# Agent attention with a maxout feed-forward layer: other ways to turn the first keys and queries, and another place in PSUM for the first product

## The chip, the cores and the metric

The kernel runs on one core of a Trainium2 chip. The time is the device time of one execution in microseconds (us). Before the change it is 464.83 us, the median of 9 runs that lie between 464.5 and 465.23.

A core has engines that work side by side, each through its own list of instructions in order: TensorE (PE in the profile, with its weight loads as PEld), VectorE (DVE), ScalarE (ACT), GpSimd (POOL) and SyncE (SP), which here only issues DMA transfers. An instruction that needs something from another engine waits for a semaphore, and everything behind it on its engine waits with it.

## The reference

Four batches of 12544 queries, keys and values of width 128 are attended through 49 agent vectors per batch, and a feed-forward layer follows.

```python
def sm(a, b):                       # softmax(scale * a @ b.T)
    ...
a2k = sm(agents, k)                 # 49 x 12544 per batch
agent_v = a2k @ v                   # 49 x 128
q2a = sm(q, agents)                 # 12544 x 49
x = (q2a @ agent_v)                 # 12544 x 128
h = max(x @ w1, x @ w2, x @ w3)     # width 768
out = h @ w_out                     # width 128
```

## The kernel before, in words

**Two streams of work.** Keys and values of a batch must be reduced completely to agent_v before any query of that batch can go on. A *key group* is nine tiles of 128 keys. A *query group*, called s in the code, is eight tiles of 128 queries; there are 49 of them. The keys of batch 0 are read first, alone, in twelve groups (ten of nine tiles and two of four). From then on query group s of one batch is worked on together with a key group of the next batch. The text calls these later key groups by the number s of the query group that hosts them: key group 0 is worked on with query group 0.

**A key group.** `load` issues two DMAs (keys, values; L275). `cast_k` and `cast_v` make bf16 of them (GpSimd, L280 and L287). `turn_k` turns the keys so that the width of 128 lies on the partitions. It does so in one of two ways: nine TensorE transposes into a PSUM tile (L294), which `evacuate` then copies to SBUF with VectorE (L300), or one transposing DMA from SBUF to SBUF issued by SP (L296). Before the change the DMA is used for s = 3 and later. Then follow the scores (L312), their exponentials (ScalarE, L317) and the product with the values (L323). The sums over key groups are kept by VectorE (L335) and, for the later batches, by GpSimd (L342).

**The end of a batch of keys.** `k_tail` divides (`normalise`: for batch 0 a reciprocal and a multiplication on VectorE, L401 and L402, which write avT) and then `product` multiplies agent_v into the weights (L418). For batch 0 that happens in two PSUM tiles. The first holds columns 768 to 1536 and is evacuated by VectorE in two parts, of 256 and 512 columns; the second holds columns 0 to 768 and is evacuated in one piece (all L423). The result is G, the weights that the queries see.

**A query group.** The queries are loaded (L474), cast (L478), turned by eight TensorE transposes (L483) and evacuated (`evacuate`, L489; for query group 0 the first half is done by ScalarE on L491). Scores (L504) and exponentials (L510) follow. For each of six slices f of the hidden width there are first(f), called u, and second(f), called v: two matmuls each on L530. `relu_first` (a, ScalarE, L545, or L542 for f = 3) and `max_second` (x, VectorE, L555, or ScalarE on L553 for f = 3) make r of them. The output is accumulated on L560 and L569, scaled by VectorE (L576) and stored (L583). The names u0, v0, a0, x0 below are these steps for slice 0.

**PSUM.** Two rings of PSUM tiles set much of the order. The ring "uv" has three tiles of two banks: products, turned keys and every u and v take one. The ring "om" has two tiles of one bank: turned queries, scores, the host tile of the key group and the outputs. A new tile waits until the reader of an older one is done.

**The order.** It is written out by hand: every step is given a key by `at`, and `emit` goes through them by key (six units of key for one query group) and puts off what lacks a predecessor or a tile. The tables KEY, LATE, BORDER and BEGIN hold the keys. `last_key` is the key of the last key group of batch 0. The order of SP's DMAs is given by the same keys. A semaphore is used again after eight DMAs, so at most eight are under way.

`keep_busy` (L254) issues matmuls whose result is not used.

Of the kernel before, what the change touches and what calls it, by code (L numbers as in the profile page):

```python
# [16 lines left out]
def kernel(  # L17
# [18 lines left out]
    nc = tc.nc  # L36
# [227 lines left out]
    def k_group(b, t0, n, key, s):  # L264

        d = {}
        early = s is None
        K = None if early else table(s)
        if s == 0:
            key += BEHIND  # L270

        def load():
            for name, src in (("k", k), ("v", v)):
                t = d[name] = load_tile()
                nc.sync.dma_start(t[:, :n, :], src[b, t0 * P:(t0 + n) * P, :].rearrange(  # L275
                    "(p j) c -> p j c", j=n))

        def cast_k():
            d["kb"] = work.tile([P, KT, C], BF16, tag="k_bf", bufs=3, name="k_bf")
            nc.gpsimd.tensor_copy(out=d["kb"][:, :n, :], in_=d["k"][:, :n, :])  # L280

        def cast_v():
            d["vb"] = work.tile([P, KT, C], BF16, tag="v_bf", bufs=4, name="v_bf")
            if early:
                nc.scalar.activation(d["vb"][:, :n, :], d["v"][:, :n, :], AF.Copy)  # L285
            else:
                nc.gpsimd.tensor_copy(out=d["vb"][:, :n, :], in_=d["v"][:, :n, :])  # L287

        def turn_k():
            d["kT"] = work.tile([P, KT, P], BF16, tag="kT", bufs=3, name="kT")  # L290
            if early or s < 3:
                t = d["kT_ps"] = uv_tile(BF16).rearrange("p i c -> p (i c)")
                for j in range(n):
                    nc.tensor.transpose(t[:, j * P:(j + 1) * P], d["kb"][:, j, :], ident)  # L294
            else:
                nc.sync.dma_start_transpose(out=d["kT"][:, :n, :],  # L296
                                            in_=d["kb"][:, :n, :].rearrange("p j c -> p (j c)"))

        def evacuate():
            nc.vector.tensor_copy(out=d["kT"][:, :n, :].rearrange("p j c -> p (j c)"),  # L300
                                  in_=d["kT_ps"][:, :n * P])

        def scores():
            if early:
                d["pair"] = uv_tile()
                d["s"] = d["pair"][:, 0, :]
                last_tile["t"] = d["s"]
            else:
                d["s"] = host[s]
            t = d["s"]  # L310
            for j in range(n):
                nc.tensor.matmul(t[:, j * A:(j + 1) * A], d["kT"][:, j, :], agT[:, b, :A],  # L312
                                 start=(j == 0), stop=True, skip_group_check=True)

        def exps():
            d["e"] = work.tile([P, KT * A], BF16, tag="e_k", bufs=3, name="e_k")
            nc.scalar.activation(d["e"][:, :n * A], d["s"][:, :n * A], AF.Exp, scale=scale)  # L317

        def values():
            t, c = (d["pair"][:, 1, :], 0) if early else (d["s"], CV)  # L320
            for j in range(n):
                e = d["e"][:, j * A:(j + 1) * A]
                nc.tensor.matmul(t[:, c:c + A], d["vb"][:, j, :], e, start=(early and j == 0),  # L323
                                 stop=True, skip_group_check=True)
                if early:
                    nc.tensor.matmul(t[:, A:2 * A], ones_bf, e, start=False, stop=True,
                                     skip_group_check=True)

        def add_values():
            w = 2 * A if early else A  # L330
            src = d["pair"][:, 1, :w] if early else d["s"][:, CV:CV + A]
            if t0 + n == NT and not early:
                nc.vector.tensor_tensor(out=avT[:, b, :A], in0=src, in1=Vacc[b], op=ALU.add)
            elif t0:
                nc.vector.tensor_tensor(out=Vacc[b], in0=src, in1=Vacc[b], op=ALU.add)  # L335
            else:
                Vacc[b] = work.tile([P, w], FP32, tag=f"Vacc{w}", name="Vacc")
                nc.vector.tensor_copy(out=Vacc[b], in_=src)

        def add_exps():  # L340
            if t0:
                nc.gpsimd.tensor_tensor(out=Eacc[b][:, :n * A], in0=Eacc[b][:, :n * A],  # L342
                                        in1=d["e"][:, :n * A], op=ALU.add)
            else:
                Eacc[b] = work.tile([P, KT * A], FP32, tag="Eacc", name="Eacc")
                nc.gpsimd.tensor_copy(out=Eacc[b], in_=d["e"])

        if early:
            g = ("early", t0)
            at(key - 30, load)  # L350
            at(key - 5, cast_k)
            at(key - 4, cast_v)
            at(key, turn_k, ("kt", g), (), "uv", [("kt_out", g)])
            at(key + 0.5, evacuate, ("kt_out", g), [("kt", g)])

            last = [("normalise", 0)] if t0 + n == NT else []
            late = max(0, (key - last_key) / 6 + 2)
            at(min(key + 6.6, last_key + 0.58 + 0.02 * late), scores, ("ks", g), [("kt_out", g)],
               "uv", [("ka", g)] + last)
            at(min(key + 7, last_key + 0.64 + 0.01 * late), exps, ("ke", g), [("ks", g)])  # L360
            done = last_key + (0.6 + 0.1 * late if late >= 1 else 0.55)
            at(min(key + 13.2, done), values, ("kv", g), [("ke", g)])
            at(min(key + 13.6, done + 0.01), add_values, ("ka", g), [("kv", g)])
        else:
            at(6.0 * s - 24.6, load)
            at(max(6.0 * s - 12.6, last_key - 3.4 + 0.2 * s), cast_k, ("k_cast", s))
            at(max(6.0 * s - 10.6, last_key - 3.3 + 0.2 * s), cast_v, ("v_cast", s))
            if s > 2:
                at(max(key - 9.1, last_key - 3.2), turn_k, ("kt_out", s), [("k_cast", s)])
            else:  # L370

                turn = 6.0 * s - 3.3 if s else KEY["v0"] + 0.01
                at(turn, turn_k, ("kt", s), (), "uv", [("kt_out", s)])
                at(turn + 0.05, evacuate, ("kt_out", s), [("kt", s)])
            at(key + K["ks"], scores, ("ks", s), [("kt_out", s), ("ho", s)])
            at(key + K["ke"], exps, ("ke", s), [("ks", s)])
            at(key + K["ke"] + 1.5, add_exps, ("kx", s), [("ke", s)])
            at(key + K["kv"], values, ("kv", s), [("ke", s), ("v_cast", s)])
            at(key + K["ka"], add_values, ("ka", s), [("kv", s)])

    def k_tail(b, sum_key, keys, s):
# [25 lines left out]
        def product(c0, *ends):  # L407

            t = uv_tile().rearrange("p i c -> p (i c)")
            a = c0  # L410
            for z in ends:
                cuts = sorted({a, z} | {c for c in (c0 + 512, C1O) if a < c < z})
                for lo, hi in zip(cuts, cuts[1:]):
                    for h in range(2):


                        c = lo + (C if lo >= C1O and h == 0 else 0)
                        nc.tensor.matmul(t[h * H:(h + 1) * H, lo - c0:hi - c0], avT[:, b, :],  # L418
                                         wall[:, c:c + hi - lo], start=True, stop=True,
                                         skip_group_check=True)  # L420
                src = t[:, a - c0:z - c0]
                if s is None:
                    nc.vector.tensor_copy(out=G[b][:, a:z], in_=src)  # L423
                else:
                    nc.scalar.activation(G[b][:, a:z], src, AF.Copy, scale=r_ag[:, b:b + 1])
                a = z
# [24 lines left out]
    def q_group(s):  # L451
# [33 lines left out]
        def evacuate():  # L485
            d["qT"] = work.tile([P, GT, P], BF16, tag="qT", bufs=3, name="qT")
            qT = d["qT"].rearrange("p j c -> p (j c)")
            half = 0 if s else GT // 2 * P
            nc.vector.tensor_copy(out=qT[:, half:], in_=d["qT_ps"][:, half:])  # L489
            if not s:  # L490
                nc.scalar.activation(qT[:, :half], d["qT_ps"][:, :half], AF.Copy)  # L491

        K = table(s)
        q_dma = s >= SB or s + 1 in tails
# [99 lines left out]
        if s == 0:  # L594
            at(last_key - 29.9, load)
            at(last_key - 3.5, cast)
            at(last_key + 0.76, turn_q, ("qt", 0), (), "om", [("qe", 0)])
            at(last_key + 0.77, evacuate, ("qe", 0), [("qt", 0)])
            at(last_key + 0.94, scores, ("s", 0), [("qe", 0)], "om", [("ex", 0)])
            at(last_key + 0.941, exps, ("ex", 0), [("s", 0)])  # L600
        elif not q_dma:
            at(key - 26, load)
            at(max(key - 12.8, last_key - 3.45 + 0.2 * s), cast, ("q_cast", s))
            put("qt", turn_q, ("q_cast", s), ring="om", frees=[("qe", s)])
            put("qe", evacuate, ("qt", s), *([("s", s - 3)] if s >= 3 else []))
# [114 lines left out]
```

The softmax here doesn't subtract the row's maximum and nothing guards it: scores larger than these inputs give would overflow.

## Time and profile before

The profiled execution took 464.95 us. Its span, from the first to the last instruction, is 463.2 us.

| quantity | value | where it is read |
|---|---|---|
| time, median of 9 runs | 464.83 us | the runs |
| profiled execution, and its span | 464.95 us, 463.2 us | the profile |
| TensorE busy | 437.7 us, 95% of the span | busy time of each engine |
| VectorE, ScalarE, GpSimd busy | 402.9, 396.2, 171.8 us | the same |
| granted TensorE clock, mean | 0.999 | clock of the core |
| keys turned by TensorE, evacuated on L300 | 15 groups, 10.7 us busy | costliest groups |
| keys turned by DMA on L296 | 30 | DMA issues |

A row of the timeline reads: start in us, duration in us, engine, line, operation, output and input tile, shapes, count. In brackets stands the time for which the engine was idle before it, and what ended that. Rows that follow each other on one engine may overlap by some hundredths of a us. A row of several instructions spans all of them. "SPq" is the time that SP spends on issuing a DMA; the time to landing is counted from the issue to the last byte.

### The profile page before, as it was taken

To read this page: it belongs to the slowest core of one execution; us is meant where nothing else is said; L and a number is where in the kernel's file an instruction comes from. 1 tells how busy PE (TensorE), PEld (TensorE's weight loads), DVE (VectorE), ACT (ScalarE), POOL (GpSimd) and SP (SyncE) were. 2 spreads that over 40 slices of the span, in tenths; PEclk is the share of its full clock that TensorE was granted. 3 is DMA by queue.
4 is the path that set the end of the run, shared out by engine and by line. 5 is a ranking of instruction groups with operands and counts; after the bars stand their busy time and mean duration, and the time that the engine had idled before them with its cause. 6 is when DMAs were issued, how large, how long until landed. Compare 5 with 4: busy or idle time off the path is not lost.

```text
span 463.2 us, 13350 instructions
## 1 busy us (share of the span) xinstructions
PE 437.7 (95%) x5473; PEld 274.3 (59%) x5473; DVE 402.9 (87%) x512; ACT 396.2 (86%) x460; POOL 171.8 (37%) x179
## 2 busy tenths in 40 slices
PE   2597899999999999999999999999999999999995
PEld 2465466666665666666656666666656555555554
DVE  3255899999988999999989999999988999999995
ACT  3465889989899899899999998998999999999991
POOL 2244963553452545536272446353240101000000
PEclk9999999999999999999999999999999999999999
DMA  8999999996999999997987999996666486644122
GB/s 311 408 411 391 409 363 323 348 323 135 323 291 304 314 266 333 292 269 226 328 306 254 281 330 295 279 266 189 174 138 187 133 193 151 174 123 124 60 93 92
DMA packets 81449, 118.26 MB, mean 255 GB/s; under 512 B 55207, under 2 KB 56683, under 8 KB 81387
## 3 DMA queue, kind: packets, MB, share of 16 engines
q1 hardware_dynamic: 81184, 117.30, 83.1%
q8 instruction: 43, 0.70, 0.6%
q14 instruction: 19, 0.16, 0.1%
q10 hardware_dynamic: 203, 0.10, 0.1%
HBM read 78.74 MB, written 25.69 MB: 225 GB/s over the span
## 4 chain that ended last, share of the span: by engine, by line
PE 80%; DMA 8%; DVE 4%; ACT 4%; issue 2%; SPq 0%; POOL 0%; DVEq 0%; ACTq 0%
PE uv_ps L530 34%; PE o_ps L569 29%; PE o_ps L560 6%; DMA st<-in_k_dram 5%; PE m_ps L483 4%; PE m_ps L504 3%; DVE r L555 3%; ACT a_sb L545 2%; DMA st<-in_q_dram 2%; DMA st<-in_v_dram 2%; PE m_ps L323 2%; PE m_ps L312 1%; PE m_ps L518 1%; DVE o_sb L576 1%; ACT uv_ps L542 0%
## 5 line engine op out<-in xcount | busy, mean ns | idle before, releaser
L555 DVE TENSOR_TENSOR r<-uv_ps,a_sb 128x1024 bf16<-128x1024 f32 x245 | 297.2, 1220 | 14.7 <-PE uv_ps L530 6.5
L545 ACT ACTIVATE a_sb<-uv_ps 128x1024 bf16<-128x1024 f32 x245 | 240.8, 1026 | 14.9 <-PE uv_ps L530 13.6
L530 PE MATMUL uv_ps<-e_q,G 49*128 49x512 bf16 (+3 forms) x1248 | 187.2, 368 | 2.5 <-ACT uv_ps L542 0.7
L569 PE MATMUL o_ps<-wo_bf,r 128*128 128x128 bf16 x2352 | 175.3, 220 | 0.2 <-DVE r L555 0.2
L569 PEld LDWEIGHTS <-r 128*128 128x128 bf16 x2352 | 137.8, 98 | 40.1 <-issue 38.2
L530 PEld LDWEIGHTS <-G 49*128 49x128 bf16 x1248 | 57.8, 93 | 65.3 <-issue 33.1
L342 POOL TENSOR_TENSOR Eacc<-Eacc,e_k 128x441 f32<-128x441 f32 (+1 forms) x30 | 30.5, 1016 | 129.4 <-ACT e_k L317 129.4
L576 DVE TENSOR_TENSOR o_sb<-o_ps,recips 128x512 f32<-128x512 f32 x98 | 67.5, 689 | 9.2 <-PE o_ps L569 6.4
L478 POOL CAST q_bf<-st 128x1024 bf16<-128x1024 f32 x49 | 51.0, 1042 | 60.8 <-DMA qT<-q_bf 59.4
L553 ACT ACTIVATE r<-uv_ps 128x1024 bf16<-128x1024 f32 x49 | 50.2, 1024 | 18.0 <-PE uv_ps L530 17.7
L280 POOL CAST k_bf<-st 128x1152 bf16<-128x1152 f32 (+2 forms) x45 | 50.7, 1127 | 27.4 <-DMA st<-in_k_dram 25.2
L542 ACT ACTIVATE uv_ps<-uv_ps 128x1024 f32<-128x1024 f32 x49 | 49.6, 1012 | 1.7 <-issue 1.3
L560 PE MATMUL o_ps<-G,e_q 128*128 128x256 bf16 x196 | 38.1, 276 | 0.3 <-DVE o_sb L576 0.3
L287 POOL CAST v_bf<-st 128x1152 bf16<-128x1152 f32 (+1 forms) x33 | 37.5, 1136 | 0.6 <-DMA st<-in_v_dram 0.6
L510 ACT ACTIVATE e_q<-m_ps 128x512 bf16<-128x512 f32 x49 | 29.8, 608 | 0.5 <-PE m_ps L504 0.5
L300 DVE COPY kT<-uv_ps 128x1152 bf16<-128x1152 bf16 (+1 forms) x15 | 10.7, 712 | 16.6 <-PE uv_ps L294 16.6
L285 ACT ACTIVATE v_bf<-st 128x1152 bf16<-128x1152 f32 (+1 forms) x12 | 12.9, 1073 | 13.4 <-DMA st<-in_v_dram 13.2
L560 PEld LDWEIGHTS <-e_q 128*128 128x128 bf16 x196 | 12.5, 97 | 19.0 <-issue 17.8
L489 DVE COPY qT<-m_ps 128x1024 bf16<-128x1024 bf16 (+1 forms) x33 | 22.2, 673 | 0.9 <-PE m_ps L483 0.9
L483 PEld LDWEIGHTS <-q_bf 128*128 128x128 bf16 x264 | 14.9, 98 | 13.3 <-issue 10.6
L483 PE MATMUL m_ps<-ident,q_bf 128*128 128x128 bf16 x264 | 20.4, 220 | 0.6 <-POOL q_bf L478 0.6
L504 PE MATMUL m_ps<-qT,agT 128*64 128x512 bf16 (+3 forms) x104 | 19.9, 388 | 0.5 <-ACT qT L491 0.5
(71 smaller groups left out, 226.9 us busy)
## 6 DMA issues: line engine op xcount, KB each, us to landing
st<-in_q_dram SPq DMA_DIRECT2D x46, 512.0 KB, 5.0
out_dram<-o_sb SPq DMA_DIRECT2D x46, 512.0 KB, 3.4
st<-in_k_dram SPq DMA_DIRECT2D x40, 576.0 KB, 6.6
st<-in_v_dram SPq DMA_DIRECT2D x40, 576.0 KB, 7.9
st<-in_k_dram SPq DMA_DIRECT2D x3, 512.0 KB, 5.6
st<-in_v_dram SPq DMA_DIRECT2D x3, 512.0 KB, 7.2
wst<-in_moe_w_dram SPq DMA_DIRECT2D x3, 384.0 KB, 10.5
st<-in_q_dram SPq DMA_DIRECT2D x2, 384.0 KB, 4.8
```

Source lines behind the costliest of these rows:

```text
L280: nc.gpsimd.tensor_copy(out=d["kb"][:, :n, :], in_=d["k"][:, :n, :])
L287: nc.gpsimd.tensor_copy(out=d["vb"][:, :n, :], in_=d["v"][:, :n, :])
L478: nc.gpsimd.tensor_copy(out=d["qb"], in_=d["q"])
L483: nc.tensor.transpose(t[:, j * P:(j + 1) * P], d["qb"][:, j, :], ident)
L530: nc.tensor.matmul(t[:, h, j0 * P:j1 * P], G[b][h * H:h * H + A, col + f * P:col + (f + 1) * P], d["e"][h * H:h * H + A, j0 * P:j1 * P], s ...
L542: nc.scalar.activation(u, u, AF.Relu)
L545: nc.scalar.activation(a_sb[f], u, AF.Relu)
L553: nc.scalar.activation(r, v_ps[f], AF.Relu)
L555: nc.vector.tensor_tensor(out=r, in0=v_ps[f], in1=a_sb[f], op=ALU.max)
L560: nc.tensor.matmul(t[:, i * 2 * C:(i + 1) * 2 * C], d["e"][:, jj * P:(jj + 1) * P], G[batch[jj]][:, C1O:C1O + 2 * C], start=(i == 0), stop ...
L569: nc.tensor.matmul(t[:, c:c + C], r_sb[f][:, h, jj * P:(jj + 1) * P], wo_bf[:, f, :], start=False, stop=True, skip_group_check=True)
L576: nc.vector.tensor_tensor(out=d["out"][:, j:j + m, :], in0=d["o", o].rearrange("p (j c) -> p j c", c=C), in1=d["r"][:, j:j + m].unsqueeze( ...
```

## The change

Five places are edited.

1. Key group 2 is turned by DMA and no longer by TensorE and VectorE. The order number of its DMA is 2.9, which puts it on SP's list behind the value load of key group 3.
2. Key group 0 is still turned by TensorE, but at `last_key + 1.05`. This is behind the two products and ahead of u0 of query group 0; before, it stood behind v0.
3. The loads of query, key and value groups 4 and 5 get later order numbers. On SP the list after the value load of key group 3 was: query 4, keys 4, values 4, query 5, keys 5, values 5, transpose 3. It becomes: transpose 2, query 4, keys 4, values 4, transpose 3, query 5, keys 5, values 5. From query 6 on the list is as it was.
4. The TensorE transposes of query group 0 stand behind the value matmuls of the last key group of batch 0 and no longer ahead of them. The evacuation of all 1024 columns is one ScalarE instruction; before, it was 512 columns on VectorE and 512 on ScalarE.
5. The first product of batch 0 is put into its PSUM tile 256 columns further on. The first part (256 columns) ends the first bank, and the second part (512 columns) fills the second bank; it is one pair of matmuls of 512 columns, where two pairs of 256 were.

```diff
 def turn_k():
-            if early or s < 3:
+            if early or s < 2:
     ...
 else:
-            at(6.0 * s - 24.6, load)
+            at(max(6.0 * s - 24.6, 6.0 * s - 21.05 if s in (4, 5) else -99), load)
     ...
-            if s > 2:
+            if s > 1:
                 at(max(key - 9.1, last_key - 3.2), turn_k, ("kt_out", s), [("k_cast", s)])
             else:
-                turn = 6.0 * s - 3.3 if s else KEY["v0"] + 0.01
+                turn = 2.7 if s else last_key + 1.05
                 at(turn, turn_k, ("kt", s), (), "uv", [("kt_out", s)])
                 at(turn + 0.05, evacuate, ("kt_out", s), [("kt", s)])
     ...
 def product(c0, *ends):
             t = uv_tile().rearrange("p i c -> p (i c)")
+            at0 = c0 if len(ends) == 1 else ends[0] - 512
             a = c0
             for z in ends:
-                cuts = sorted({a, z} | {c for c in (c0 + 512, C1O) if a < c < z})
+                cuts = sorted({a, z} | {c for c in (at0 + 512, C1O) if a < c < z})
     ...
-                        nc.tensor.matmul(t[h * H:(h + 1) * H, lo - c0:hi - c0], avT[:, b, :],
+                        nc.tensor.matmul(t[h * H:(h + 1) * H, lo - at0:hi - at0], avT[:, b, :],
     ...
-                src = t[:, a - c0:z - c0]
+                src = t[:, a - at0:z - at0]
     ...
 def evacuate():                          # of a query group
-            half = 0 if s else GT // 2 * P
-            nc.vector.tensor_copy(out=qT[:, half:], in_=d["qT_ps"][:, half:])
-            if not s:
-                nc.scalar.activation(qT[:, :half], d["qT_ps"][:, :half], AF.Copy)
+            if s:
+                nc.vector.tensor_copy(out=qT, in_=d["qT_ps"])
+            else:
+                nc.scalar.activation(qT, d["qT_ps"], AF.Copy)
     ...
 if s == 0:
-            at(last_key + 0.76, turn_q, ("qt", 0), (), "om", [("qe", 0)])
-            at(last_key + 0.77, evacuate, ("qe", 0), [("qt", 0)])
+            at(last_key + 0.802, turn_q, ("qt", 0), (), "om", [("qe", 0)])
+            at(last_key + 0.803, evacuate, ("qe", 0), [("qt", 0)])
 elif not q_dma:
-            at(key - 26, load)
+            at(key - (21.08 if s in (4, 5) else 26), load)
```

## The prediction

> **What bounds the kernel now.** First the page's head, then the busy time by stage: the hand-over from the keys of batch 0 to the first queries (41.3 to 51.0), the first query groups (51.0 to 62.6), and later groups.
>
> ```profile
> span 463.2 us, 13350 instructions
> PE 437.7 (95%) x5473; PEld 274.3 (59%) x5473; DVE 402.9 (87%) x512; ACT 396.2 (86%) x460; POOL 171.8 (37%) x179
> ...
> core 0: us, PE busy (x) PEld busy (x) DVE busy (x) ACT busy (x) POOL busy (x), PEclk, DMA share, GB/s
> 41.30:51.00 9.70, 7.43 (x85) 3.80 (x81) 6.52 (x12) 4.80 (x7) 7.62 (x8) 1.00 1.02 408
> 51.00:60.00 9.00, 8.13 (x101) 4.49 (x99) 7.80 (x12) 8.11 (x12) 8.17 (x9) 1.00 1.02 409
> 71.00:79.35 8.35, 8.35 (x109) 5.33 (x110) 8.01 (x11) 7.63 (x10) 4.19 (x4) 1.00 1.13 304
> ```
>
> From about 63 us a query group takes 8.35 us and TensorE is busy for all of it. No edit touches a group after s = 3, so nothing is won there: a stretch that TensorE fills is only moved as a whole. The change can win where TensorE stands idle, in the 21 us from 41.3 to 62.7. There the chain of waits and the timeline say what ends each wait:
>
> ```profile
> 42.68 0.44 DVE qT L489
> ...
> 43.14 0.61 ACT qT L491
> ...
> 44.42 0.43 DVE G L423
> ...
> 47.99 0.76 DVE L300 COPY kT<-uv_ps 128x1152 bf16<-128x1152 bf16 x1 [1.09 <-PE uv_ps L294]
> 48.66 1.21 DVE L555 TENSOR_TENSOR r<-uv_ps,a_sb 128x1024 bf16<-128x1024 f32 x1
> 49.24 1.01 ACT L542 ACTIVATE uv_ps<-uv_ps 128x1024 f32<-128x1024 f32 x1 [1.31 <-issue]
> 51.66 0.66 PE L294 MATMUL uv_ps<-ident,k_bf 128*128 128x128 bf16 x9 [0.34 <-DVE r L555]
> ...
> 61.32 0.76 DVE L300 COPY kT<-uv_ps 128x1152 bf16<-128x1152 bf16 x1 [0.79 <-PE uv_ps L294]
> 61.99 0.68 DVE L576 TENSOR_TENSOR o_sb<-o_ps,recips 128x512 f32<-128x512 f32 x1
> 62.73 0.39 PE L560 MATMUL o_ps<-G,e_q 128*128 128x256 bf16 x2 [0.27 <-DVE o_sb L576]
> 63.83 0.39 PE L312 MATMUL m_ps<-agT,kT 128*128 128x49 bf16 x9
> ```
>
> Two spots are seen. At 47.99 VectorE gets to the keys of group 0 only after 1.09 idle, x0 stands behind them (48.66), and ScalarE waits 1.31 for u3. At 61.32 VectorE waits 0.79 for the keys of group 2, evacuates them, and only then scales the output (61.99) for which TensorE waits at 62.73.
>
> **The change part by part.** Times are places in the trace of before.
>
> *First queries.* They arrive as before: the cast ends at 41.96, the eight transposes at 42.64. The two halves of the evacuation run one after the other (0.42 and 0.60), to 43.74. One ScalarE instruction of 128x1024 takes 1.02 by the row of L553: 42.68 to 43.70. The scores start at 43.76 and not 43.79. The values of the last key group move from 42.48 to about 41.3, so VectorE has avT long before it is needed; before, it came at 44.02, just ahead of the product at 44.08. The product follows the scores by 0.22 (512 columns): 43.98, so 0.09 is won.
>
> *First product.* Its first part is evacuated from 44.33 to 44.75. The second part waited 0.5 for that evacuation before (44.42 plus 0.43, then TensorE at 44.90). Here the Trainium skill speaks: PSUM — Partial Sum Buffer, section "PSUM bank collisions raise a hardware error", has PSUM guarded by bank and quadrant. In another bank the second part then needs no wait. But in the program as built it still carries one: for VectorE's instruction behind the one that writes avT, which is this evacuation. I go by the program: TensorE at 44.81 (44.75 plus the 0.05 of a semaphore), end 45.22, evacuations of 512 and 768 columns from 45.24 and 45.85 (0.69 and 0.95 by their rows), end 46.79. Without the wait these would start about 0.5 earlier.
>
> *Keys of group 0.* The nine transposes stand behind the second product, which ends issuing at 45.35; the cast of these keys ends at 44.81 (43.66 plus 1.15), so they need not wait. On PSUM's ring u0 and u1 now take the tiles of the products, so u0 waits for the evacuation that ends at 45.93, and a0 starts at 46.40 where it was 45.99. This loss of 0.41 lies in ScalarE's idle 1.31: a1 ends at 48.34 instead of 47.93, and u3, no longer behind two fillers and eight transposes, is there at 48.15. So a3 starts at 48.36 (was 49.24). VectorE copies the keys at 46.73 without a wait, v0 takes their tile at 47.54, and x0 starts at 47.95 (was 48.66). x0 decides: behind it stand the evacuation of query group 1, x1, and the keys of group 1 at 51.66, which wait for x1. All move by 0.71. ScalarE gains 0.88 at a3 and is held to the same by these keys, whose tile u5 takes. **First sum: 0.7.** It is 0.3 if some wait in this chain has been missed by me (the 0.41 of a0 not hidden), 1.2 if the second part doesn't wait.
>
> *Keys of group 2.* Nine matmuls (nine weight loads from 60.56, so 0.48 of TensorE's issue) and one VectorE copy of 0.76 go. VectorE is free at 60.53 and TensorE's part for L576 ends at 60.78, so the scaling runs 60.8 to 61.5 and L560 can go at 61.5 (was 62.73). u4 and v2 of query group 1 follow at once. But v4 needs the tile of a4, and ScalarE is full from 59.74: x3, a2, a4 (1.02, then 2.01 for two) end at 62.65. So v4 goes at 62.67 where it was 63.27 (the second pair of 63.06). From there TensorE is without a gap, with u0 of the next group held by a5 at 64.17 (due at 64.2). **Second sum: 0.6.** Its ends: 0.3 (ScalarE's wait of 0.33 at a5 is all that is won) and 0.75 (x4 and x5 gain more).
>
> *The DMAs.* These rows are issues of SP, with the time to landing of the two transposes:
>
> ```profile
> 54.55 0.33 SPq L275 DMA_DIRECT2D st<-in_v_dram  x1
> 57.22 5.24 SPq L296 DMA_TRANSPOSE kT<-k_bf  x1
> 67.43 2.10 SPq L296 DMA_TRANSPOSE kT<-k_bf  x1
> ...
> DMA to landing us min/median/max: 9.6/9.6/9.6
> ...
> DMA to landing us min/median/max: 7.7/7.7/7.7
> ```
>
> Transpose 2 waits for its cast (51.90 plus 1.15) and so goes at 53.1; SP, behind the value load of 46.28, holds back query 4 (47.71 before) until then. By that time the eight loads under way still have to 57.3 to go (loads of this stretch land after about 11 us), so the DMA engines don't run dry. What a transpose adds to them: the first landed at 66.8, 1.15 after the load ahead of it (54.55 plus 11.1); the second at 75.1, 2.46 after the store ahead (66.97 plus 5.7). The skill's Advanced Engine Details and Errata, section "X-Bar Transpose (TRN2)", calls transposes as fast as plain DMAs: 295 KB at 410 GB/s would be 0.72, an estimate. The rows count, 1.15 to 2.46. So transpose 2 lands at 58.5 to 59.8, and its scores, at 63.83 before, are due at 62.5. It pushes all behind it by 1.15 to 2.46: query 4 lands near 60.0 (cast at 59.21 before, used 15 us later), keys 4 near 61.4 (cast by 62.6; GpSimd's list keeps its order, and behind that cast stands L342, due at 63.8 where it was 65.09), transpose 3 at 64 to 66 (due 70.9), transpose 4 at 76.3 to 77.6 instead of 75.1 (its scores, 80.53 before, are due at 79.2). By the page's figure it would be 75.9. Price nothing; least cover 1.6.
>
> *Sum.* 0.7 + 0.6 = 1.3 off the span of 463.2: 461.9. The profiled execution lies 1.75 above its span, and 0.12 above the median: 463.65 and **463.5 us** for the median, 0.28% below 464.83. Within 0.2% (0.93 us) a measurement of this kernel can't be told from no change.
>
> **The rivals.**
>
> *The wait between the product's parts is gone after all.* For it: the second part lies in another bank. Against: the wait in the program. VectorE starts the 512 columns at 44.75 (not 45.24): first sum 1.2, time 463.0.
>
> *Only one spot pays.* ScalarE has 8.11 of 9.00 busy between the spots; if a0's 0.41 or the order of tiles isn't hidden, the first sum is 0 to 0.3 with the second 0.3 to 0.6. Against it: the idle 1.31 on ScalarE behind a1. Time about 464.2, no change by measure.
>
> *Transpose 2 comes too late*, the case on the other side. TensorE holds its whole list at the scores of key group 2, and later groups can't win it back. It costs its landing less 62.5. At 63.83 both gains are gone, which is 10.7 in flight after 53.1; from 64.8 (11.7) on it is slower by more than 0.2%. For it: 9.6 in flight for the transpose of 57.22, behind seven loads, and 11 for loads of this stretch. Against: only three or four loads are ahead of it. At 12.0 in flight, in the middle of this case, it lands at 65.1, costs 2.6 and the time is 466.1. The same loss falls at 80.53 if two transposes take five us more of the DMA engines than seen.
>
> **How the numbers follow.** The sum as worked out 0.50; no wait between the parts 0.12; one spot only 0.22; late transpose 0.16, two thirds of it slower by over 0.2%, else no change. With the edge of the likeliest (0.8 to 1.7, so 463.1 to 464.0) a little of it falls within 0.2% too: faster 0.60, same 0.28, slower 0.12. The range for 8 in 10 goes from 462.8, below the gone wait, to 465.2, into the late transpose.
>
> **What would show it.** Right: x0 (L558 then) near 47.95 and a3 near 48.36, a0 later than before near 46.40, no L294 row behind 52, lin1 of query group 0 (L560, L563 after) near 61.5 less 0.7, so 60.8, the scores of key group 2 without a wait for a DMA, and 8.35 per group behind that. Wrong: TensorE starts the product's second part ahead of 44.8, or waits at L312 on a DMA of kT near 62 or 79, or GpSimd's casts wait for queries 4 or 5 long enough to hold up the sums of L342.

## The result and the profile after

The changed kernel takes 463.34 us (median of 10 runs, 462.89 to 464.45); the kernel before, run beside it, takes 464.92 us (30 runs). The ratio is 0.9966, with a 95% interval of 0.9958 to 0.9974: faster by 0.34%. The forecast was 463.5 us, in a range of 462.8 to 465.2. A second measurement of the changed kernel, told below, gave 463.38 us and 0.9967 (0.9955 to 0.9979).

The profiled execution after took 463.36 us. These are the head of its page and its busy time by engine, and then the busy time in the same three stretches as before (columns as in the prediction):

```profile
span 461.6 us, 13325 instructions
...
PE 437.1 (95%) x5462; PEld 273.8 (59%) x5462; DVE 402.5 (87%) x510; ACT 396.7 (86%) x460; POOL 171.7 (37%) x179
```

```profile
core 0: us, PE busy (x) PEld busy (x) DVE busy (x) ACT busy (x) POOL busy (x), PEclk, DMA share, GB/s
41.30:51.00 9.70, 7.34 (x87) 3.84 (x84) 6.76 (x12) 6.04 (x8) 7.61 (x8) 1.00 1.02 409
51.00:60.00 9.00, 8.34 (x98) 4.77 (x98) 7.67 (x12) 7.93 (x12) 7.72 (x9) 1.00 1.11 341
71.00:79.35 8.35, 8.35 (x112) 5.33 (x110) 8.01 (x11) 7.63 (x10) 4.19 (x4) 1.00 1.11 334
```

The busy time has hardly changed: TensorE has 0.6 us less, VectorE 0.4. The span is 1.6 shorter, so most of what went is idle time of TensorE. The later groups take 8.35 us as before, with TensorE busy for all of it. The timeline after, with the rows that answer to those shown of before:

```profile
46.37 1.94 ACT L548 ACTIVATE a_sb<-uv_ps 128x1024 bf16<-128x1024 f32 x2 [1.70 <-PE uv_ps L533]
46.59 0.75 DVE L300 COPY kT<-uv_ps 128x1152 bf16<-128x1152 bf16 x1
...
48.09 1.23 DVE L558 TENSOR_TENSOR r<-uv_ps,a_sb 128x1024 bf16<-128x1024 f32 x1 [0.75 <-PE uv_ps L533]
...
48.28 1.01 ACT L545 ACTIVATE uv_ps<-uv_ps 128x1024 f32<-128x1024 f32 x1
...
51.11 0.66 PE L294 MATMUL uv_ps<-ident,k_bf 128*128 128x128 bf16 x9 [0.54 <-DVE r L558]
...
60.27 0.69 DVE L579 TENSOR_TENSOR o_sb<-o_ps,recips 128x512 f32<-128x512 f32 x1 [0.29 <-PE o_ps L572]
...
61.04 0.39 PE L563 MATMUL o_ps<-G,e_q 128*128 128x256 bf16 x2
...
62.12 0.39 PE L533 MATMUL uv_ps<-e_q,G 49*128 49x512 bf16 x2 [0.36 <-ACT a_sb L548]
...
62.67 0.39 PE L312 MATMUL m_ps<-agT,kT 128*128 128x49 bf16 x9
```

VectorE's idle 1.09 ahead of the keys of group 0 is gone (46.59 has no bracket), and ScalarE's 1.31 ahead of a3 too (48.28). But x0, which sets what follows, starts at 48.09 and behind a new idle time of 0.75: VectorE now has the keys early and waits for v0. The keys of group 1, which wait for x1, follow at 51.11 (51.66 before). In the second spot the scaling no longer stands behind a key copy, and lin1 starts at 61.04 (62.73 before). The scores of key group 2 (62.67) have no bracket: they wait for no DMA. v4 at 62.12 is held by a4, as the prediction said.

The chain of waits after, in the first spot (start, duration, what):

```profile
44.19 0.44 DVE G L426
...
44.67 0.42 PE uv_ps L421 x2
...
45.11 1.57 DVE G L426 x2
...
46.72 0.39 PE uv_ps L533 x2
47.12 0.54 PE m_ps L254 x2
47.65 0.34 PE uv_ps L533 x2
...
48.09 1.23 DVE r L558
```

The second part of the product (44.67) still waits for the first part's evacuation (44.19 to 44.63). Behind the evacuations the chain does not go through the key copy. It goes through TensorE's list: u1 (46.72), two matmuls of `keep_busy` (47.12), v0 (47.65), x0.

Where the time went, by the starts of the exponentials of query groups (the row of e_q), in two profiled executions of each kernel:

| stretch, us | before | before again | after | after again |
|---|---|---|---|---|
| span start to group 0 | 44.23 | 44.37 | 44.08 | 44.00 |
| group 0 to 1 (first spot) | 9.38 | 9.38 | 8.98 | 8.98 |
| group 1 to 3 (second spot) | 17.84 | 17.85 | 17.23 | 17.21 |
| group 3 to 46 | 355.06 | 355.15 | 354.76 | 354.74 |
| group 46 to 48 | 15.73 | 15.72 | 15.72 | 15.72 |
| group 48 to the end | 20.96 | 20.83 | 20.83 | 20.85 |

The two spots give 0.40 and 0.61 to 0.63. Another 0.3 to 0.4 lies between groups 3 and 46, where no step was edited (0.3 of it in two groups, told at the end of the experiments). The rest lies at the end and in when the first queries arrive, which differs by a tenth or more from one execution to the next (they landed at 40.87 in the profile of before and at 40.76 in that of after).

### The profile page after: what moved, and what is told of

Same layout as the page of the kernel before. It is cut to its first block, busy times and chain, and to the rows that moved or that the text cites. A ratio compares the mean times of both kernels' runs of the same rounds, so it can differ in the third digit from the quotient of the medians.

```text
span 461.6 us, 13325 instructions
## 1 busy us (share of the span) xinstructions
PE 437.1 (95%) x5462; PEld 273.8 (59%) x5462; DVE 402.5 (87%) x510; ACT 396.7 (86%) x460; POOL 171.7 (37%) x179
## 4 chain that ended last, share of the span: by engine, by line
PE 80%; DMA 8%; DVE 5%; ACT 4%; issue 1%; SPq 0%; POOL 0%; DVEq 0%; ACTq 0%
PE uv_ps L533 34%; PE o_ps L572 29%; PE o_ps L563 6%; DMA st<-in_k_dram 5%; PE m_ps L486 4%; DVE r L558 4%; PE m_ps L507 3%; ACT a_sb L548 2%; DMA st<-in_q_dram 2%; DMA st<-in_v_dram 2%; PE m_ps L323 2%; PE m_ps L312 1%; PE m_ps L521 1%; DVE o_sb L579 0%; DVE G L426 0%
## 5 line engine op out<-in xcount | busy, mean ns | idle before, releaser
L533 PE MATMUL uv_ps<-e_q,G 49*128 49x512 bf16 (+3 forms) x1248 | 186.7, 368 | 2.6 <-DVE G L426 0.4
L572 PE MATMUL o_ps<-wo_bf,r 128*128 128x128 bf16 x2352 | 175.3, 220 | 0.2 <-DVE r L558 0.2
L572 PEld LDWEIGHTS <-r 128*128 128x128 bf16 x2352 | 137.8, 98 | 40.0 <-issue 38.1
L533 PEld LDWEIGHTS <-G 49*128 49x128 bf16 x1248 | 57.7, 93 | 64.7 <-issue 32.9
L556 ACT ACTIVATE r<-uv_ps 128x1024 bf16<-128x1024 f32 x49 | 50.2, 1024 | 18.0 <-PE uv_ps L533 17.7
L492 DVE COPY qT<-m_ps 128x1024 bf16<-128x1024 bf16 x32 | 21.8, 681 | 0.0
```

The source lines that it names most:

```text
L533: nc.tensor.matmul(t[:, h, j0 * P:j1 * P], G[b][h * H:h * H + A, col + f * P:col + (f + 1) * P], d["e"][h * H:h * H + A, j0 * P:j1 * P], s ...
L556: nc.scalar.activation(r, v_ps[f], AF.Relu)
L572: nc.tensor.matmul(t[:, c:c + C], r_sb[f][:, h, jj * P:(jj + 1) * P], wo_bf[:, f, :], start=False, stop=True, skip_group_check=True)
```

## The experiments

**One part of the change alone.** Three kernels, each the kernel before with one edit. The first has edits 1 and 3, so the keys of group 2 by DMA and the new order of loads.

```diff
-            if early or s < 3:
+            if early or s < 2:
     ...
-            at(6.0 * s - 24.6, load)
+            at(max(6.0 * s - 24.6, 6.0 * s - 21.05 if s in (4, 5) else -99), load)
     ...
-            if s > 2:
+            if s > 1:
     ...
-            at(key - 26, load)
+            at(key - (21.08 if s in (4, 5) else 26), load)
```

> The kernel before with the keys of group 2 turned by DMA and the loads of groups 4 and 5 behind it, nothing else. The reckoning (two separate gains): 0.6 us faster than before; all starts up to 59 us as before, lin1 of query group 0 (L560) near 61.5 and no longer 62.7, exponentials of query group 3 0.6 us earlier. If the two spots are not separate but one gain seen twice: nothing, or all of the 1.6 us, here. If the DMA order costs something: less than 0.3 us.

Measured: 463.7 us beside 464.78, ratio 0.9977 (0.997 to 0.9984). In the trace the second spot is shorter by 0.63 (17.21), and the first as before (9.38). The time fell by 1.08, where 0.6 was expected: 0.45 more than the stretch explains.

The second has edit 2 for group 0 alone.

```diff
-                turn = 6.0 * s - 3.3 if s else KEY["v0"] + 0.01
+                turn = 6.0 * s - 3.3 if s else last_key + 1.05
```

> The kernel before with the transposes of key group 0 put ahead of u0, nothing else. The reckoning: 0.4 to 0.6 us faster; a0 later by 0.4 (near 46.4), u3's relu (L542) earlier by 0.8, x0 near 48.2 and no longer 48.66. If the later a0 isn't hidden by ScalarE's idle 1.3 us: no change or slower by up to 0.4 us.

Measured: 464.7 us beside 464.78, ratio 1.0001 (0.9993 to 1.0009). The trace has a gain in its place, 9.06 for the first spot (0.32 less, where 0.4 to 0.6 was expected), but the time does not show it. Two groups far behind, 15 and 39, are longer by 0.23 and 0.36 in this trace, and two that are long in the kernel before (0.14 and 0.16) are not: together 0.29 lost, which all but takes up the 0.32. Why is told with the last experiment.

The third has edit 4 alone, the first queries.

```diff
-            half = 0 if s else GT // 2 * P
-            nc.vector.tensor_copy(out=qT[:, half:], in_=d["qT_ps"][:, half:])
-            if not s:
-                nc.scalar.activation(qT[:, :half], d["qT_ps"][:, :half], AF.Copy)
+            if s:
+                nc.vector.tensor_copy(out=qT, in_=d["qT_ps"])
+            else:
+                nc.scalar.activation(qT, d["qT_ps"], AF.Copy)
     ...
-            at(last_key + 0.76, turn_q, ("qt", 0), (), "om", [("qe", 0)])
-            at(last_key + 0.77, evacuate, ("qe", 0), [("qt", 0)])
+            at(last_key + 0.802, turn_q, ("qt", 0), (), "om", [("qe", 0)])
+            at(last_key + 0.803, evacuate, ("qe", 0), [("qt", 0)])
```

> The kernel before with the first queries turned behind the last values and evacuated by one ScalarE instruction, nothing else. The reckoning: 0.1 us or less; VectorE writes avT near 42.7 and no longer 44.0, but the product stays behind the scores on TensorE (near 44.0). If the path runs over VectorE and avT: more than 0.5 us faster.

Measured: 464.66 us beside 464.78, ratio 0.9999 (0.9991 to 1.0008): no change to be measured. In the trace the exponentials of group 0 start 3.32 after the landing of the queries (3.36 before), and the first spot takes 9.30 (9.38): 0.12 together. So at equal arrival the first spot is worth 0.32 + 0.12 = 0.44, and the second 0.61 to 0.63. The changed kernel itself agrees: 3.32 from the landing to the exponentials of group 0, and 8.98 for the first spot, 0.04 and 0.40 less than before.

**The banks.** The changed kernel with the first product back at its old place in PSUM (edit 5 undone).

```diff
-            at0 = c0 if len(ends) == 1 else ends[0] - 512
+            at0 = c0
```

> The changed kernel with the first product at its old place in PSUM (two pairs of 256 columns, the first of them in the bank that VectorE reads). The reckoning: the time of the changed kernel within 0.1 us, because the wait for the first part's evacuation is there in both. If the other bank is what wins: 0.5 us slower than the changed kernel, and TensorE's idle time ahead of the second part shows only here.

Measured: 463.13 us, ratio 0.9968 (0.9956 to 0.998), not to be told from the changed kernel. Its chain of waits:

```profile
44.06 0.43 DVE G L426
...
44.54 0.42 PE uv_ps L421 x4
```

The second part starts 0.48 after the start of the first evacuation, here in the same bank; in the changed kernel, in another bank, it is also 0.48 (44.19, 44.67). Both spots are as long as in the changed kernel (8.98 and 17.21). The place within the tile is worth nothing. The next kernel puts the first part into a PSUM tile of its own, from the other ring.

```diff
+            first = t if len(ends) == 1 else small_tile("m_ps")
     ...
-                        nc.tensor.matmul(t[h * H:(h + 1) * H, lo - at0:hi - at0], avT[:, b, :],
+                        nc.tensor.matmul((first if z == ends[0] else t)[h * H:(h + 1) * H, lo - at0:hi - at0], avT[:, b, :],
     ...
-                src = t[:, a - at0:z - at0]
+                src = (first if z == ends[0] else t)[:, a - at0:z - at0]
```

> The changed kernel with the first part (256 columns) of the first product in a PSUM tile of its own, so that nothing makes the second part wait for its evacuation. The reckoning: TensorE has the second part 0.1 us behind the first and not 0.6; VectorE's copies of 512 and 768 columns, u1, v0, x0 and all behind it move by 0.5 us; 0.5 us faster than the changed kernel. If another chain (ScalarE's from a0, or the keys of group 1) holds x0: less than 0.2 us.

Measured: 462.89 us, ratio 0.9957 (0.9944 to 0.9969). Its chain of waits:

```profile
44.20 1.90 DVE G L426 x3
...
46.14 0.39 PE uv_ps L533 x2
46.53 0.54 PE m_ps L254 x2
47.07 0.34 PE uv_ps L533 x2
...
47.50 1.23 DVE r L558
```

The three evacuations now run as one piece of 1.90, and VectorE waits for TensorE nowhere between them; x0 starts at 47.50, and the first spot takes 8.38: 0.60 less than in the changed kernel. In the changed kernel the second part lies in another bank of the same tile and waits; in another tile it does not. So the wait goes with the tile, not with the bank.

**The fillers.** The changed kernel without the two matmuls of `keep_busy` between u1 and v0.

```diff
-    for key, n in fillers + [(last_key + 0.9, 2), (KEY["u1"] + 0.01, 2),
+    for key, n in fillers + [(last_key + 0.9, 2),
```

> The changed kernel without the two matmuls of no use that stand between u1 and v0 of query group 0. The reckoning: v0 then waits for the copy of the keys of group 0, which ends at 47.34, and starts at 47.4 and not 47.6; 0.2 us faster than the changed kernel. If the two matmuls were needed to hold TensorE's clock: a granted clock under 1.00 behind 46 us and a slower kernel.

Measured: 463.1 us, ratio 0.9966 (0.9953 to 0.9978). Its chain of waits, in an execution in which the first evacuation started 0.22 later than in the changed kernel's (44.41, 44.19):

```profile
45.33 1.55 DVE G L426 x2
46.88 0.68 DVE kT L300
...
47.60 0.41 PE uv_ps L533 x2
...
48.10 1.23 DVE r L558
```

Now the chain goes through the key copy (46.88), and v0 follows its end. x0 starts 3.69 after the first evacuation (3.90 in the changed kernel), and the first spot takes 8.78, 0.20 less. The timed difference (0.24) lies within the intervals; the trace settles it. The granted clock stays at 1.00 from 41 to 60 us, so in this execution the fillers were not needed for it.

**Both together.** The own tile, and no fillers.

> The changed kernel with both: the first part in its own tile, and no matmuls of no use between u1 and v0. The reckoning: the gains add, 0.6 to 0.7 us faster than the changed kernel, 2.0 to 2.3 us faster than before. If one chain holds both: no more than 0.5.

Measured: 462.67 us, ratio 0.9954 (0.9941 to 0.9966): the lowest time of all. The first spot takes 8.20, 0.78 less than in the changed kernel: 0.60 and 0.20 add up.

**The changed kernel again.**

> The changed kernel once more. By the two gains that the traces show (0.44 and 0.63, with the same arrival of the first queries): 1.1 us faster than before. By the first measurement: 1.6 us. What is beyond 1.1 lies outside the edited stretch and should show as differences in single executions, not at one place.

Measured: 463.38 us, ratio 0.9967 (0.9955 to 0.9979), with the same stretches (table above).

**Where transpose 2 stands on SP's list.** The changed kernel with edit 3 undone: the transpose of the keys of group 2 stands behind query 4, keys 4 and values 4.

```diff
-            at(max(6.0 * s - 24.6, 6.0 * s - 21.05 if s in (4, 5) else -99), load)
+            at(6.0 * s - 24.6, load)
     ...
-            at(key - (21.08 if s in (4, 5) else 26), load)
+            at(key - 26, load)
```

> The changed kernel with the loads of key groups 4 and 5 and of the queries 4 back at their earlier places: on SP's list the transpose of the keys of group 2 now stands behind the query load 4 and the loads of keys and values 4, instead of ahead of them. Theory (the transpose's DMA time is what it adds behind the loads under way; the cover is a few microseconds): the three loads are 1.7 MB, about 4.1 us at 410 GB/s, so it lands at about 62.4 (58.3 plus 4.1), and its scores stand at 62.67: the cover is used up, the scores of key group 2 wait for 0 to 0.7 us, and the kernel takes 463.3 to 464.1 us. Rival (the place among the loads is worth nothing, since the cover is wide): 463.3 to 463.4 us and no wait for a DMA at the scores (L312).

Measured: 463.76 us beside 465.0, ratio 0.9976 (0.9966 to 0.9987). The transpose is issued at 52.92 and lands 9.4 later, at 62.3 (62.4 was expected). Its scores start at 62.63 and do not wait; both spots are as in the changed kernel (8.98 and 17.22). So the cover is nearly used up, 0.3 is left, but in the profiled execution, the fastest of the seven (463.44), nothing is lost. The median is 0.4 above that of the changed kernel, but the two ratios have intervals that overlap. Whether the transpose comes too late in some of the slower executions is not shown.

The next kernel has this edit too and issues the transpose later still, behind keys and values 5.

```diff
-                at(max(key - 9.1, last_key - 3.2), turn_k, ("kt_out", s), [("k_cast", s)])
+                at(max(key - 9.1, last_key - 3.2) + (3.1 if s == 2 else 0), turn_k, ("kt_out", s), [("k_cast", s)])
```

> As the run above, with the transpose of the keys of group 2 issued later by one group of loads, just ahead of the transpose of group 3: it stands behind the loads of keys and values 5 too. Theory (a late transpose stops TensorE's whole list at the scores of key group 2, and no later group wins it back): it lands near 67, so TensorE waits 4 to 5 us at L312, all of it stays, and the kernel takes 467 to 468.5 us, slower than before. Rival (what is lost is won back, since the later query groups have slack): below 465 us.

Measured: 470.31 us beside 465.0, ratio 1.011 (1.0096 to 1.0124): slower than before, and 7.0 us above the changed kernel, 2.8 more than the wait explains. Its chain of waits, and its busy time and granted clock (the column PEclk) by stretch:

```profile
55.97 11.12 DMA kT<-k_bf
...
67.14 0.56 PE m_ps L312 x9
67.70 0.85 PE o_ps L572 x8
68.55 1.40 PE uv_ps L533 x6
```

```profile
core 0: us, PE busy (x) PEld busy (x) DVE busy (x) ACT busy (x) POOL busy (x), PEclk, DMA share, GB/s
...
63.00:67.00 4.00, 0.00 (x0) 0.00 (x0) 0.97 (x1) 0.60 (x1) 0.00 (x0) 0.87 1.20 207
67.00:69.00 2.00, 1.86 (x21) 1.39 (x23) 0.00 (x0) 0.54 (x1) 0.58 (x1) 0.50 1.07 364
69.00:71.00 2.00, 2.00 (x17) 1.16 (x14) 1.23 (x1) 1.44 (x2) 2.00 (x3) 0.50 1.06 430
71.00:73.00 2.00, 2.00 (x26) 1.15 (x24) 1.43 (x4) 0.63 (x2) 1.60 (x2) 0.55 0.39 156
73.00:75.00 2.00, 2.00 (x28) 1.36 (x26) 2.00 (x3) 1.44 (x2) 0.00 (x0) 1.00 1.01 302
```

The transpose lands at 67.1, as the theory had it, and TensorE waits 4.17. But then it goes on at half its granted clock: eight matmuls of L572 take 0.85 and six of L533 1.40 (0.45 and 0.78 on the chain of the changed kernel), and the granted clock is 0.50 from 67 to 71, back at 1.00 from 73. From the scores at 67.14 to the turning of the next queries at 72.77 are 5.63 us; in the changed kernel the same work takes 3.17 (62.67 to 65.84). The wait and this loss of 2.46 make 6.6, and the second spot is longer by 6.74 (23.97). Nothing of it is won back: groups 3 to 46 take 354.87 (354.76 in the changed kernel). The rival falls, and the theory had the wait right and left the clock out.

**One more DMA, and the kernel before once more.** These two ask for the part of the gain that lies outside the two spots. The first is the kernel before with a small load into a buffer that nothing reads.

```diff
+    extra = const.tile([A, B, C], FP32, name="extra")
+    at(9.95, lambda: nc.sync.dma_start(extra, agents.rearrange("b a c -> a b c")))
```

> The kernel before with one more small DMA on SP (100 KB into a buffer that nothing reads), right behind the transpose of the keys of group 3. No other instruction is moved. The kernels that turn the keys of group 2 by DMA were measured about 0.45 us faster than the shorter stretches in their traces explain, and their traces end 0.5 us sooner behind the last scaling of the output (4.3 us against 4.8 and 4.7). Theory A (one more DMA gives the last store another of the eight DMA semaphores, which SP waits for sooner in its final list): 464.3 to 464.5 us and an end of 4.3 us behind the last scaling. Theory B (the extra is not of the count of DMAs): 464.8 to 464.9 us and an end as before.

> The kernel before, profiled a second time, for its end and for the two groups that were 0.14 and 0.16 us longer in its first trace. If these belong to the kernel: 4.8 us from the last scaling to the end again, and query groups 8 and 23 longer again. If they are chance of one execution: an end of 4.3 us may come, and other groups are longer.

Measured: with the extra DMA 464.75 us beside 465.0, ratio 0.9993 (0.9984 to 1.0001). The interval holds both theories, so the time alone does not decide. In the trace 4.5 pass from the start of the last scaling to the end; theory A wanted 4.3. Counted from the exponentials of the last query group, the end is nearly the same in all of them: 20.83 to 20.96 before and after (table above), 20.74 with the extra DMA. So theory A's 0.5 at the end is not there to be explained; counting from the last scaling alone had misled.

The second profile of the kernel before (465.05 us) shows where the difference is. Groups 8 and 23 are longer than in the changed kernel by 0.13 and 0.16 again, where the first profile had 0.14 and 0.16, and the kernel with the extra DMA has 0.13 and 0.16 in the same groups. In group 8 it is six matmuls. The chain of the kernel before, second profile, and then of the changed kernel:

```profile
114.48 0.45 PE o_ps L569 x8
114.93 0.90 PE uv_ps L530 x6
```

```profile
113.16 0.45 PE o_ps L572 x8
113.61 0.78 PE uv_ps L533 x6
```

The chain names no wait, but VectorE's rows have one. These are its last scaling ahead of these matmuls and the maxima (the x of the slices) behind that, in the kernel before (second profile) and in the changed kernel:

```profile
112.01 0.69 DVE L576 TENSOR_TENSOR o_sb<-o_ps,recips 128x512 f32<-128x512 f32 x1
113.03 1.22 DVE L555 TENSOR_TENSOR r<-uv_ps,a_sb 128x1024 bf16<-128x1024 f32 x1 [0.33 <-PE m_ps L504]
114.17 1.22 DVE L555 TENSOR_TENSOR r<-uv_ps,a_sb 128x1024 bf16<-128x1024 f32 x1
```

```profile
110.69 0.69 DVE L579 TENSOR_TENSOR o_sb<-o_ps,recips 128x512 f32<-128x512 f32 x1
111.35 1.23 DVE L558 TENSOR_TENSOR r<-uv_ps,a_sb 128x1024 bf16<-128x1024 f32 x1
```

In the kernel before, the maximum at 113.03 starts 0.33 after VectorE has become free, although its a and v were both done by 112.57; the bracket names the scores (L504), which it does not read. The next maximum therefore ends at 115.39, and the last two of the six matmuls, which wait for it, start at 115.44. In the changed kernel the first maximum follows the scaling at once. The same holds for the other long groups: in 8 and 23 of the kernel before and of the one with the extra DMA, and in 15 and 39 of the one with edit 2 alone, a maximum of VectorE starts 0.27 to 0.37 late with nothing left to wait for, and a pair of TensorE starts 0.05 behind the end of it or of the next one.

Where these maxima stand in VectorE's list is no chance. Counted from 0, with its waits, in the order of the trace, they are entries 191 and 447 in the kernel before and with the extra DMA (lists of 853), and 319 and 703 with edit 2 alone (854). All are 63 more than a multiple of 128. In every other kernel here the list has 852 entries, such places fall on other instructions, and no group from 3 to 46 is longer than in the changed kernel by more than 0.02. One of the places, entry 831, is again a maximum in the changed kernel, and it too is 0.35 late, in the last group. So the late starts belong to the program as built, and a list of another length moves them. What happens at these entries was not tested. VectorE waiting for its code would fit, by an estimate. The page of before has a queue of instructions with 0.70 MB; if it serves TensorE, that is 64 bytes for each of its 10946 matmuls and weight loads, and the packets of the other such queue (19 with 0.16 MB) hold about 130 instructions each.

The late starts account for 0.3 of the gain of the changed kernel, and for most of the 0.45 left over in the first experiment. For the kernel with edit 4 alone the times don't confirm it: it has none in these groups either, and was only 0.12 faster; its end is 0.28 longer in the trace (21.24 from group 48), and its interval reaches to 0.4 faster.

## Why the prediction was right

**The sum.** The prediction had 0.7 and 0.6; the traces show 0.44 and 0.61 to 0.63, so 1.05 to 1.07 where 1.3 was forecast. That 463.5 came out near 463.34 is luck in part: the 0.3 from late starts of VectorE, which no step of it knew of, made up for the short first sum. The rest of the measured 1.58, about 0.2, has no sure place. In the first pair of profiles it is 0.11 of earlier arrival and 0.13 at the end, but two executions of one kernel differ by as much. The line of 0.2% below which nothing can be told was drawn too wide: most intervals here reach about 0.1% to each side.

**First queries.** 0.09 was forecast for the start of the product; alone the edit gives 0.12. Right.

**First product.** The prediction followed the program, in which the second part waits, and set aside what one might conclude from the Trainium skill, which has PSUM guarded by bank and quadrant (PSUM — Partial Sum Buffer, section "PSUM bank collisions raise a hardware error"). The trace has that wait in both places (0.48), and only a tile of its own takes it away. The sign of being wrong, a start ahead of 44.8, came by the letter (44.67), but by the earlier arrival (0.11) and not because the wait was gone. The rival in which it is gone needed a first sum of 1.2. With the own tile the first spot is worth 0.44 + 0.60 = 1.04: nearly that, but from another edit.

**Keys of group 0: the term that was mis-sized.** The prediction had v0 taking the tile of the key copy at 47.54, and x0 at 47.95. In the trace x0 is at 48.09, in an execution in which the queries arrived 0.11 earlier, so 0.25 later than forecast. The step overlooked is TensorE's own list: u1 waits for the last evacuation (46.72), two fillers stand between it and v0, and v0 begins at 47.65. Without the fillers the chain is the one that the prediction drew, through the key copy, and it gains 0.20 more. That makes the first spot 0.64, close to the 0.7. The other steps of this part hold: a0 at 46.37 (46.40 forecast, 46.29 at the earlier arrival), its loss hidden in ScalarE's idle time, and a3 at 48.28 (48.36, or 48.25).

**Keys of group 2.** Right as drawn. lin1 starts at 61.04 (60.8 forecast); v4 waits for a4, and starts 0.55 ahead of the 62.67 of the second sum, which is what the first spot gave (0.44, and 0.11 by the arrival). The second sum of 0.6 is set by a4 and not by the removed copy: lin1 itself has moved by 1.69.

**The DMAs.** This is SP's part of the timeline after, and then the time to landing of the three transposes, in the same order:

```profile
52.98 1.34 SPq L296 DMA_TRANSPOSE kT<-k_bf  x1
...
57.10 2.08 SPq L296 DMA_TRANSPOSE kT<-k_bf  x1
...
66.28 6.33 SPq L296 DMA_TRANSPOSE kT<-k_bf  x1
```

```profile
kT<-k_bf SPq DMA_TRANSPOSE x1, 5.3
...
kT<-k_bf SPq DMA_TRANSPOSE x1, 8.4
...
kT<-k_bf SPq DMA_TRANSPOSE x1, 11.2
```

They land at 58.3, 65.5 and 77.5. The forecast was 58.5 to 59.8, 64 to 66, and 76.3 to 77.6, so the first came 0.2 ahead of its range and the others within theirs. For the last, the rows of before, read as 1.15 to 2.46 of DMA time for a transpose, were the better guide than the Trainium skill (Advanced Engine Details and Errata, section "X-Bar Transpose (TRN2)"), which calls transposes as fast as regular DMAs: by the estimate made from that it would have landed at 75.9. The packets in the trace of before agree with the rows: a transpose of keys has 1152 of 256 bytes, which took 32 ns each in the mean, so 2.3 us over the 16 DMA engines. The price of nothing was right, with 4.4 us of cover for the first.

**The rivals.** "Only one spot pays" did not come. "Transpose 2 too late" is real from its place on: with the loads of group 4 ahead of it the cover shrinks to 0.3, and with those of group 5 too the kernel is slower than before. Edit 3 is what keeps the distance. But the price that the prediction put on it, landing less due time, was too low. For a landing at 67.1 it gives 4.6 of loss, while TensorE waited 4.17 and 6.7 were lost in that spot, most of the rest because the clock fell.

## What to carry to other kernels

When an edit takes work out of the way of an engine, read the other engine's list between the two points as well: what stands there in program order, fillers too, becomes the next limit. A wait between two parts of one PSUM tile may come from the tile and not from the memory; giving the parts different tiles is a cheap trial. Before a gain of 0.3% is put down to an edit, compare the stretches that the edit does not touch: here a fifth of the gain came from there, where VectorE's late starts went with a list that was one entry shorter.

## What the runs showed of the hardware

**The price of a long wait of TensorE.** A wait of 4.17 us cost 6.6. TensorE had been idle since 62.97; the granted clock was 0.99 from 65.0 to 66.0, 0.50 from 66.0 to 66.5, still 0.50 from 72.4 to 72.8, and 0.98 from 72.8 to 73.2. The Trainium skill (TensorE: Matmul & The Clock Gate, section "What's actually happening") has two states, half clock after an idle window of about 3.4 us and full clock after about 3.4 us of sustained work, the window running freely. The fall after about 3 us agrees roughly. The return took 5.7 us from the first matmul. By an estimate from the page's 3.4, windows that end at 66.0, 69.4 and 72.8 would fit both, if one that is partly idle does not count. That is argued, not shown.

**What a transpose does to SP.** Issuing one held SP for 1.34, 2.08 and 6.33 us in the changed kernel, for 5.23 in the kernel with the loads of group 4 first, and for 9.58 for two in a row in the late one; the plain loads between 46 and 66 us of the changed kernel took 0.33 to 0.65 of it.

**Late starts of VectorE at fixed places of its list.** A maximum of VectorE started 0.27 to 0.37 us late with nothing left to wait for that the trace shows, each time at an entry that is 63 more than a multiple of 128, and TensorE waited for it where it had no slack: 0.3 together in the kernel before and 0.59 in the one with edit 2 alone, where all edits of this change gain 1.05.
